# The recurrence's joint visits taken apart into the steps around them, and the decay rows spread over the partitions

## Chip, cores and metric

The kernel runs on one core of one Trainium2 chip. The metric is the device time of one execution in microseconds, the median over several; smaller is better.

## What is computed

A retention recurrence feeds a two-layer network. Batch 4, 8 heads, 768 tokens, head width 64; the network goes from 512 to 2048 and back to 512, on all 3072 tokens. The weights are handed over in double precision and made into fp32 on the chip.

```python
gamma = 1.0 - 2.0 ** (-5.0 - np.arange(H))
for t in range(S):
    state = gamma * state + einsum('bhd,bhe->bhde', k[:, :, t], v[:, :, t])
    y[:, :, t] = scale * einsum('bhd,bhde->bhe', q[:, :, t], state)
x = y.transpose(0, 2, 1, 3).reshape(B * S, H * D)
h = x @ w_in
g = np.maximum(0.01 * h, h)
out = g @ w_out
```

## The kernel before

**Chunks.** The 768 tokens are cut into NC = 6 chunks of 128 (`c`); each has 4 batches (`b`). For a chunk and batch the recurrence is a few small products on TensorE. `score` multiplies k by q into two PSUM banks (64x64 tiles of the array, four at a time); `masked` multiplies by the causal mask on VectorE. `decay_v` multiplies v by a power of the decay, on GpSimd, or on ScalarE and VectorE at the start. `reads` multiplies the state by q, `values` the masked scores by v, into the same two banks (`yp`); `state` multiplies k by v for the state's next value, into an unused part of those banks. `tokens_taken` moves the result into the network's input `x`, and `state_taken` adds the sums to the state and multiplies it by the decay; both are VectorE.

**The network.** Each matrix product is done with seven block products instead of eight (`seven`, steps M1, M6, M5, M4, M2, M7, M3), which land in the PSUM banks A, B, C, D, A, B, C of a ring of four (tag "ff"). `hidden(c, u)` is the first layer for a quarter `u` of the 2048 columns, `output` the second. A step of one part is 8 records of a 128x256 product on TensorE; in chunks 2 to 5 `output` takes two parts and 16 records. After each step VectorE or ScalarE empties the bank (`takes`): in `hidden`, M1 and M5 are copied by ScalarE, M6 is added by VectorE, M7 brings three VectorE adds and M3 one, and then the four differences of `g`. The seven products need differences of `x` as well (`differences`: four VectorE subtractions into `t` and `x[1]`); M1 needs none of them, M6 the second, M5 the first, M4 the third, M7 the changed `x[1]`.

**Order.** The order on every engine is that of the program text: each engine and each DMA queue works its list from front to back, and waits at an entry until what it depends on is done. `run(steps, at)` goes through the seven steps of a part and calls what `at` lists behind a step. Chunks 0 and 1 are worked together, unit by unit, while the weights arrive and are converted; chunks 2 to 5 follow one by one, each in two pairs of units (hidden, hidden, output).

**Where the recurrence of chunks 2 to 5 stands.** Behind chunk 0's last output part's steps 0 and 3 stand the scores and the rest for batches 0 and 1 of chunk 2 (`scored`, `visit`); step 4 of chunk 1's has the scores of batches 2 and 3. From then on `visit_with_scores` stands behind an output part: the scores of the next pair of batches (`score_apart`, each batch into two "ff" banks) between the reads, values and sums of the present pair, whose sums go into an "ff" bank of their own (`states_apart`). Where a chunk is completed by a visit, the differences of its `x` lie in it too. The last pair of batches has `visit` in output step 3.

**Loads.** SP's queue issues the loads of q and k (`ahead`, once the reads have let go of the old ones), then those of k and v (`load_kv`, at the visit's end), then the stores of the output parts. Batches 2 and 3 have their q and k in a free output tile.

**The start.** The decay tables come as 8 rows of 780 numbers in partitions 0 to 7 (`rows`, part of `t`), on ScalarE's DMA queue, and are spread over the partitions by products of 8 rows (`tables`, `spread`) into `dec`. Before data arrives TensorE multiplies zeros (`keep_busy`, from `nothing`, a 256-column strip of `t` set to zero by VectorE).

Of the kernel before, what the change touches and what calls it, by code (L numbers as in the profile page):

```python
# [23 lines left out]
def kernel(  # L24
# [143 lines left out]
    turn = [0]  # L168

    def new_am(c, b):  # L170

        i = turn[0]
        turn[0] = (i + 1) % (3 if (c, b) >= (2, 2) else 2)
        if i < 2:
            return work.tile([128, 2, HP, C], FP32, tag=f"am{i}", name=f"am_{c}_{b}")
        place = new_t(1, f"am_{c}_{b}").rearrange("p i k n -> p (i k n)")[:, 0 : 2 * HP * C]
        return place.rearrange("p (j a t) -> p j a t", j=2, a=HP)

    def new_t(c, name):
        return work.tile([128, 3, 2, N], FP32, tag=f"t{int(c == 1)}", name=name)  # L180

    def new_o(c, name="o"):
        return work.tile([128, 4, 2, N], FP32, tag=f"o{int(c > 0)}", name=f"{name}_{c}")

    def masked(c, b):
        am = new_am(c, b)
        nc.vector.tensor_tensor(
            out=am.rearrange("p j a t -> p (j a) t"),
            in0=scores[c, b].rearrange("p j a t -> p (j a) t"),
            in1=mask.unsqueeze(1).to_broadcast([128, H, C]), op=ALU.mult)  # L190
        scores[c, b] = am
# [25 lines left out]
    def state(c, b):  # L217
        y = heads[c, b][1]
        sp = for_state(sums_at[c, b])
        for a in range(HP) if c < NC - 1 else ():  # L220
            sums_of(sp, y, a)
# [24 lines left out]
    def taken(c, b, xb):  # L246

        tokens_taken(c, b, xb)
        state_taken(c, b, for_state(sums_at[c, b]))
# [7 lines left out]
    def state_taken(c, b, sp):  # L257
        sums_at.pop((c, b))
        if 0 < c < NC - 1:
            nc.vector.tensor_tensor(out=st[b], in0=st[b], in1=sp, op=ALU.add)  # L260
            nc.vector.tensor_tensor(out=st[b], in0=st[b],
                                    in1=gc.unsqueeze(2).to_broadcast([128, HP, D]), op=ALU.mult)

    def ahead(c, b):


        if c >= NC:
            return
        if b < 2:
            x = work.tile([128, 2, HP, C], FP32, tag="qk", bufs=AHEAD, name=f"qk_{c}_{b}")  # L270
        else:
            if b == 2:
                room[c] = new_o(0).rearrange("p i k n -> p (i k n)")
            x = room[c][:, ds((b - 2) * 2 * HP * C, 2 * HP * C)]
            x = x.rearrange("p (s a t) -> p s a t", s=2, a=HP)
        heads[c, b] = [x, None]
        load_qk(c, b)

    def load_kv(c, b):
        y = work.tile([128, 2, H, D], FP32, tag="kv", bufs=AHEAD, name=f"kv_{c}_{b}")  # L280
        heads[c, b][1] = y
        nc.sync.dma_start(out=y, in_=kv[c, b])

    room = {}

    def score_apart(c, b):

        x = heads[c, b][0]
        ps = scores[c, b] = [psum.tile([128, HP, C], FP32, tag="ff", bufs=4, name=f"ap{j}_{c}_{b}")
                             for j in range(2)]  # L290
        for a in range(HP):
            for u in range(2):
                for j in range(2):
                    nc.tensor.matmul(ps[j][ts(u, 64), a, :], lhsT=x[ts(j, 64), 1, a, ts(u, 64)],  # L294
                                     rhs=x[ts(j, 64), 0, a, :])

    def masked_apart(c, b, j):
        if j == 0:
            weights_of[c, b] = new_am(c, b)
        nc.vector.tensor_tensor(out=weights_of[c, b][:, j], in0=scores[c, b][j],  # L300
                                in1=mask.unsqueeze(1).to_broadcast([128, HP, C]), op=ALU.mult)
        if j == 1:
            scores[c, b] = weights_of.pop((c, b))

    weights_of = {}

    def states_apart(c, b):

        ps = psum.tile([128, 2, HP, D], FP32, tag="ff", bufs=4, name=f"sp_{c}_{b}")
        for i in range(2):  # L310
            y = heads.pop((c, b + i))[1]
            for a in range(HP):
                sums_of(ps[:, i], y, a, start=(i == 0 and a == 0))
        return ps

    def visit(c, b):

        for f in (reads, values, state):
            for i in range(2):
                f(c, b + i)  # L320
        for i in range(2):
            tokens_taken(c, b + i, xs[c][0])
        for i in range(2):
            state_taken(c, b + i, for_state(sums_at[c, b + i]))
        for i in range(2):
            if c + 1 < NC:
                ahead(c + 1, b + i)

    def visit_with_scores(c, b, following, complete=False):

        x = xs[c][0]
        early, late = ((following[0], following[1] + i) for i in range(2))
        score_apart(*early)
        for i in range(2):
            reads(c, b + i)
        masked_apart(*early, 0)
        masked_apart(*early, 1)
        score_apart(*late)  # L340
        for i in range(2):
            values(c, b + i)
        masked_apart(*late, 0)
        for i in range(2):
            tokens_taken(c, b + i, x)
        sp = states_apart(c, b)
        if complete:
            if xs[c][1] is None:
                xs[c][1] = new_t(c, f"t_{c}")
            t = xs[c][1]  # L350
            for k in range(2):
                minus(t[:, 0, k], x[:, 1, k], x[:, 0, k])
                minus(t[:, 1, k], x[:, 3, k], t[:, 0, k])
        masked_apart(*late, 1)
        if complete:
            minus(t[:, 2], x[:, 2], t[:, 1])
            last_difference(x)
        for i in range(2):
            state_taken(c, b + i, sp[:, i])
        for i in range(2):  # L360
            ahead(c + 1, b + i)
        for at in (early, late):
            load_kv(*at)
        for at in (early, late):
            decay_v(*at)
# [126 lines left out]
    def last_difference(x):  # L492
        minus(x[:, 1], x[:, 3], x[:, 1])
# [3 lines left out]
    FIRST = (0, 4, 1, 2, 3, 5, 6)  # L497
# [148 lines left out]
    def new_x(c):  # L646
        x = tile_x(c)
        return [x, new_t(c, f"t_{c}") if c < 3 else None]
# [22 lines left out]

    def differ(c):
        def do():
            if xs[c][1] is None:
                xs[c][1] = new_t(c, f"t_{c}")
            differences(*xs[c])
        return do
# [12 lines left out]
    place_for(0, 2, new_o(0, "in"))  # L690
    place_for(0, 3, new_o(1, "in"))
# [3 lines left out]
    rows = t[0:H, 1:3].rearrange("p i k n -> p (i k n)")[:, 0 : decay.shape[1]]  # L695
    nc.scalar.dma_start(out=rows, in_=decay)
# [27 lines left out]
    nothing = t[:, 0, 0, :].bitcast(BF16)  # L724
    nc.vector.memset(t[:, 0, 0, :], 0.0)
    idle = psum.tile([128, 2, N], FP32, tag="ff", bufs=4, name="idle")

    def keep_busy(n):
        for _ in range(n):
            nc.tensor.matmul(idle.rearrange("p i n -> p (i n)"), lhsT=nothing[:, 0:128],  # L730
                             rhs=nothing, start=True, stop=True, skip_group_check=True)
# [8 lines left out]
    keep_busy(7)  # L740
# [6 lines left out]
    nc.vector.tensor_copy(out=dec[:, n_gq:], in_=tables[:, 0, 0 : H + HP])  # L747
# [3 lines left out]
    decay_v(0, 0, nc.vector)  # L751
# [77 lines left out]
    later = hidden(1, 0, x1, t1, *parts[1][1:], order=FIRST)  # L829
# [9 lines left out]
    state_taken(1, 2, for_state(sums_at[1, 2]))  # L839
    state_taken(1, 3, for_state(sums_at[1, 3]))  # L840
# [4 lines left out]
    for u in range(NU):  # L845
# [5 lines left out]
        for c in range(2):  # L851
# [5 lines left out]
            if u == NU - 1 and NC > 2:  # L857
                if c == 0:
                    xs[2] = new_x(2)
                if c == 0:  # L860
                    at = {0: [scored(2, 0), scored(2, 1)], 3: [lambda: visit(2, 0)]}
                else:
                    at = {1: [lambda: ahead(2, 2), lambda: ahead(2, 3)],
                          2: [lambda: load_kv(2, 2), lambda: load_kv(2, 3)],
                          4: [scored(2, 2), scored(2, 3)]}
            run(output(c, os[c], [parts[c]], u == 0, u == NU - 1), at)

    if NC > 2:
        visit_with_scores(2, 2, (3, 0), complete=True)
    for c in range(2, NC):  # L870
        os[c] = new_o(c)
        for p in range(NU // 2):
            pair = []
            for u in (2 * p, 2 * p + 1):
                pair.append(new_g(c, u))
                run(hidden(c, u, *xs[c], *pair[-1][1:]), {})
            last = p == NU // 2 - 1
            at = {}
            if c + 2 == NC and last:
                at = {3: [lambda: visit(c + 1, 2)], 5: [differ(c + 1)]}  # L880
            run(output(c, os[c], pair, p == 0, last), at)

            if c + 1 < NC and p == 0:
                xs[c + 1] = new_x(c + 1)
                visit_with_scores(c + 1, 0, (c + 1, 2))
            elif c + 2 < NC and last:
                visit_with_scores(c + 1, 2, (c + 2, 0), complete=True)
# [83 lines left out]
```

## Time and profile before

| | |
|---|---|
| median of 3 runs | 667.42 us (666.89 to 667.49) |
| the profiled execution | 667.42 us, span 665.4 us |
| TensorE matmul, busy | 658.7 us |
| TensorE weight load, busy | 574.2 us |
| VectorE, busy | 372.1 us |
| ScalarE, busy | 176.2 us |
| GpSimd, busy | 18.5 us |
| granted TensorE clock | 1.00 |
| moved by DMA | 48.92 MB, mean 74 GB/s |

The span is the time from the first to the last instruction that the profiler shows; the execution's time has some 2 us around it. Busy time is the union of an engine's instructions. Matmuls overlap in the array, so that a row's busy time is longer than the distance between starts. In the timeline a row has: start in us, busy time in us, engine, line, operation, output<-inputs, shape, how many were merged, and in brackets the idle time of the engine before the row with what ended it. PE is TensorE, DVE VectorE, ACT ScalarE, POOL GpSimd; SPq is SP's DMA queue.

### The profile page before, as it was taken

Reading aid. Unit: us, or ns where it says so; the run is one execution under the profiler, and the core shown is the slowest. Engines: PE = TensorE matmul, PEld = TensorE weight load, DVE = VectorE, ACT = ScalarE, POOL = GpSimd, SP = SyncE. Lnnn points to the kernel's source line nnn. Section 1 sums busy time; section 2 is a strip of 40 time slices with the busy share of each in tenths; the row PEclk is TensorE's granted clock in tenths of the full one; section 3 lists DMA queues with packets and bytes.
Section 4 is the critical chain, followed back from the end, with each engine's and each line's share of the span. In section 5 each row is a group of like instructions: output and inputs, shape, how many; then the busy total and the mean of one; then the engine's idle time right before and its main releaser. Section 6 shows DMA issues by size and latency. Waiting matters only on the chain.

```text
span 665.4 us, 10517 instructions
## 1 busy us (share of the span) xinstructions
PE 658.7 (99%) x4537; PEld 574.2 (86%) x4537; DVE 372.1 (56%) x588; ACT 176.2 (26%) x322; POOL 18.5 (3%) x22
## 2 busy tenths in 40 slices
PE   8999999999999999999999999999999999999998
PEld 5888888888888888888888888888888888888886
DVE  5789969889888684243437414527333343431342
ACT  5854555264261002202102211300220210221210
POOL 0000000000000020001001001001000100000000
DMA  8920312313222640030022003004000101000001
GB/s 325 398 103 33 126 64 76 115 65 109 113 83 86 222 182 1 0 116 12 1 93 99 1 1 127 1 16 176 1 0 23 42 1 43 22 0 1 1 0 63
DMA packets 15757, 48.92 MB, mean 74 GB/s; under 512 B 1752, under 2 KB 2008, under 8 KB 15712
## 3 DMA queue, kind: packets, MB, share of 16 engines
q1 hardware_dynamic: 15696, 48.24, 20.0%
q8 instruction: 35, 0.57, 0.4%
q14 instruction: 10, 0.08, 0.0%
q10 hardware_dynamic: 16, 0.02, 0.0%
HBM read 41.97 MB, written 6.29 MB: 73 GB/s over the span
## 4 chain that ended last, share of the span: by engine, by line
PE 95%; DVE 2%; DMA 1%; SPq 0%; issue 0%
PE B_o L521 13%; PE A_o L521 13%; PE C_o L521 12%; PE A_h L521 12%; PE C_h L521 11%; PE B_h L521 11%; PE D_o L521 6%; PE D_h L521 6%; PE yp L210 3%; PE d L543 2%; PE ap L294 2%; PE ap L165 1%; PE yp L201 1%; DMA in<-in_qk_dram 1%; DVE t L470 1%; PE sp L225 1%
## 5 line engine op out<-in xcount | busy, mean ns | idle before, releaser
L521 PE MATMUL A_h<-x,w 128*128 128x256 f32 x368 | 87.7, 381 | 0.0
L521 PEld LDWEIGHTS A_h<-x,w 128*128 128x128 f32 x368 | 69.3, 190 | 9.7 <-issue 0.2
L521 PE MATMUL A_o<-g,w 128*128 128x256 f32 x288 | 68.1, 379 | 0.0
L467 DVE TENSOR_TENSOR m<-m,B_h 128x512 f32<-128x512 f32 x23 | 15.8, 687 | 90.8 <-PE B_h L521 90.8
L521 PEld LDWEIGHTS A_o<-g,w 128*128 128x128 f32 x288 | 54.6, 190 | 7.6 <-issue 0.2
L561 ACT COPY m<-A_h 128x512 f32<-128x512 f32 x23 | 13.5, 586 | 175.8 <-PE A_h L521 155.5
L556 ACT ACTIVATE g<-g 128x512 f32<-128x512 f32 x69 | 42.0, 629 | 66.0 <-DVE g L467 66.0
L467 DVE TENSOR_TENSOR m<-m,B_o 128x512 f32<-128x512 f32 x16 | 11.0, 685 | 64.3 <-PE B_o L521 64.3
L521 PE MATMUL D_h<-t,w 128*128 128x256 f32 x184 | 43.7, 380 | 0.7 <-DVE states L260 0.6
L521 PE MATMUL C_h<-x,w 128*128 128x256 f32 x184 | 43.5, 379 | 0.0
L521 PE MATMUL C_h<-t,w 128*128 128x256 f32 x184 | 43.5, 379 | 0.0
L521 PE MATMUL B_h<-t,w 128*128 128x256 f32 x184 | 43.5, 379 | 0.0
L521 PE MATMUL B_h<-x,w 128*128 128x256 f32 x184 | 43.5, 379 | 0.0
L521 PEld LDWEIGHTS D_h<-t,w 128*128 128x128 f32 x184 | 34.7, 190 | 6.4 <-PE C_h L521 1.8
L521 PEld LDWEIGHTS C_h<-x,w 128*128 128x128 f32 x184 | 35.0, 190 | 4.8
L521 PEld LDWEIGHTS C_h<-t,w 128*128 128x128 f32 x184 | 35.0, 190 | 4.8
L521 PEld LDWEIGHTS B_h<-t,w 128*128 128x128 f32 x184 | 35.0, 190 | 4.8
L521 PEld LDWEIGHTS B_h<-x,w 128*128 128x128 f32 x184 | 35.0, 190 | 4.7
L470 DVE TENSOR_TENSOR gd<-g,gd 128x512 f32<-128x512 f32 x48 | 33.2, 692 | 1.7
L521 PE MATMUL C_o<-gd,w 128*128 128x256 f32 x144 | 34.0, 379 | 0.0
L521 PE MATMUL B_o<-gd,w 128*128 128x256 f32 x144 | 34.0, 379 | 0.0
L521 PE MATMUL B_o<-g,w 128*128 128x256 f32 x144 | 34.0, 379 | 0.0
(125 smaller groups left out, 999.5 us busy)
## 6 DMA issues: line engine op xcount, KB each, us to landing
raw<-in_weights_dram SPq DMA_DIRECT2D x31, 512.0 KB, 4.3
kv<-in_kv_dram SPq DMA_DIRECT2D x17, 512.0 KB, 4.7
out_dram<-o SPq DMA_DIRECT2D x23, 256.0 KB, 2.3
qk<-in_qk_dram SPq DMA_DIRECT2D x11, 512.0 KB, 3.6
o<-in_qk_dram SPq DMA_DIRECT2D x8, 512.0 KB, 3.3
in<-in_qk_dram SPq DMA_DIRECT2D x5, 512.0 KB, 8.6
in<-in_kv_dram SPq DMA_DIRECT2D x3, 512.0 KB, 8.4
kv<-in_kv_dram SPq DMA_DIRECT2D x4, 256.0 KB, 7.2
```

The costliest lines, as they stand in the source:

```text
L165: nc.tensor.matmul(ps[ts(u, 64), j, a, :], lhsT=x[ts(j, 64), 1, a, ts(u, 64)], rhs=x[ts(j, 64), 0, a, :])
L201: nc.tensor.matmul(ps[ts(i, 64), j, m, :], lhsT=st[b][ts(j, 64), a, :], rhs=x[ts(j, 64), 0, a, :], start=(m == 0), stop=False, skip_group_ ...
L210: nc.tensor.matmul(ps[ts(i, 64), j, m, :], lhsT=y[:, 1, 2 * a + j, :], rhs=am[:, j, a, :], start=(c == 0 and m == 0), stop=True, skip_grou ...
L225: nc.tensor.matmul(sp[ts(j, 64), a, :], lhsT=y[:, 0, 2 * a + j, :], rhs=y[:, 1, 2 * a + j, :], start=start, stop=True, skip_group_check=True)
L294: nc.tensor.matmul(ps[j][ts(u, 64), a, :], lhsT=x[ts(j, 64), 1, a, ts(u, 64)], rhs=x[ts(j, 64), 0, a, :])
L467: nc.vector.tensor_tensor(out=out, in0=a, in1=b, op=ALU.add)
L470: nc.vector.tensor_tensor(out=out, in0=a, in1=b, op=ALU.subtract)
L521: nc.tensor.matmul(half, lhsT=block(w, sa)[:, k, ts(i, 128)], rhs=rhs[:, k, :], start=(first and (i == 0 or split) and n == 0 and k == 0), ...
L543: nc.tensor.matmul(banks[r][:, i, :], lhsT=block(2 * u, r + 2 * kh)[:, k, ts(i, 128)], rhs=x[:, 2 * kh + th, k, :], start=(step == 0 and i ...
L556: nc.scalar.activation(g[:, i], g[:, i], AF.Prelu, alpha=0.01)
L561: nc.scalar.copy(out=got["m1"], in_=ps)
```

## The change

The joint visits go. For each chunk from 2 on, the scores of a pair of batches stand behind one step and reads, values, sums, tokens and state behind a later one: in output steps 0 and 3 of chunks 0 and 1 for chunk 2, and in steps 1 and 4 of the first hidden part of each pair for chunks 3 to 5. Both use the two-bank tiles (tag "att"). The loads of the pair after the next two batches are issued right behind a read, q and k and then k and v for each batch. The differences of chunk 2 stand in output step 4 of chunk 1, the others in output step 1 of the second pair.

At the start the 8 rows lie in partitions 0, 16, 32 and so on, and GpSimd and VectorE first set all 128 partitions of that strip to zero, so that the products that spread them run over 128 rows. `nothing` is 64 columns wide, set before all else on VectorE; eight products of zeros stand at the front in place of seven. ScalarE copies the small table to `dec`, and GpSimd makes the first `decay_v`.

```diff
-    def visit(c, b):
+    def products(c, bs):
         for f in (reads, values, state):
-            for i in range(2):
-                f(c, b + i)
...
+            for b in bs:
+                f(c, b)
+
+    def stage_y(c, bs, xb):
+        products(c, bs)
+        for b in bs:
+            taken(c, b, xb)
+            n = c * B + b + AHEAD
+            if c > 1 and n < NC * B:
+                load(*divmod(n, B))
...
-    def visit_with_scores(c, b, following, complete=False):
...
+    def read(c, *bs):
+        return lambda: stage_y(c, bs, xs[c][0])
...
-    rows = t[0:H, 1:3].rearrange("p i k n -> p (i k n)")[:, 0 : decay.shape[1]]
-    nc.scalar.dma_start(out=rows, in_=decay)
+    rows = t[:, 1:3].rearrange("p i k n -> p (i k n)")[:, 0 : decay.shape[1]]
+    nothing = t[:, 0, 0, 0:64].bitcast(BF16)
+    nc.vector.memset(t[:, 0, 0, 0:64], 0.0)
+    half = decay.shape[1] // 2
+    nc.gpsimd.memset(rows[:, :half], 0.0)
+    nc.vector.memset(rows[:, half:], 0.0)
+    nc.scalar.dma_start(out=rows[0 : 128 : 128 // H], in_=decay)
...
-    nothing = t[:, 0, 0, :].bitcast(BF16)
-    nc.vector.memset(t[:, 0, 0, :], 0.0)
...
-            nc.tensor.matmul(idle.rearrange("p i n -> p (i n)"), lhsT=nothing[:, 0:128],
-                             rhs=nothing, start=True, stop=True, skip_group_check=True)
+            nc.tensor.matmul(idle.rearrange("p i (two n) -> p (i two) n", two=2), lhsT=nothing,
+                             rhs=nothing.unsqueeze(1).to_broadcast([128, 4, 128]),
+                             start=True, stop=True, skip_group_check=True)
...
-    keep_busy(7)
+    keep_busy(8)
...
-    nc.vector.tensor_copy(out=dec[:, n_gq:], in_=tables[:, 0, 0 : H + HP])
+    nc.scalar.copy(out=dec[:, n_gq:], in_=tables[:, 0, 0 : H + HP])
...
-    decay_v(0, 0, nc.vector)
+    decay_v(0, 0)
...
-                if c == 0:
-                    at = {0: [scored(2, 0), scored(2, 1)], 3: [lambda: visit(2, 0)]}
-                else:
-                    at = {1: [lambda: ahead(2, 2), lambda: ahead(2, 3)],
-                          2: [lambda: load_kv(2, 2), lambda: load_kv(2, 3)],
-                          4: [scored(2, 2), scored(2, 3)]}
+                at = {0: [scored(2, 2 * c), scored(2, 2 * c + 1)],
+                      3: [read(2, 2 * c, 2 * c + 1)]}
+                if c == 1:
+                    put(at, s4=[differ(2)])
             run(output(c, os[c], [parts[c]], u == 0, u == NU - 1), at)
-    if NC > 2:
-        visit_with_scores(2, 2, (3, 0), complete=True)
     for c in range(2, NC):
+        more = c + 1 < NC
         os[c] = new_o(c)
+        if more:
+            xs[c + 1] = new_x(c + 1)
         for p in range(NU // 2):
             pair = []
             for u in (2 * p, 2 * p + 1):
                 pair.append(new_g(c, u))
-                run(hidden(c, u, *xs[c], *pair[-1][1:]), {})
-            last = p == NU // 2 - 1
-            at = {}
-            if c + 2 == NC and last:
-                at = {3: [lambda: visit(c + 1, 2)], 5: [differ(c + 1)]}
-            run(output(c, os[c], pair, p == 0, last), at)
-            if c + 1 < NC and p == 0:
-                xs[c + 1] = new_x(c + 1)
-                visit_with_scores(c + 1, 0, (c + 1, 2))
-            elif c + 2 < NC and last:
-                visit_with_scores(c + 1, 2, (c + 2, 0), complete=True)
+                at = {}
+                if more and u == 2 * p:
+                    at = {1: [scored(c + 1, u), scored(c + 1, u + 1)],
+                          4: [read(c + 1, u, u + 1)]}
+                run(hidden(c, u, *xs[c], *pair[-1][1:]), at)
+            at = {1: [differ(c + 1)]} if p == 1 and more else {}
+            run(output(c, os[c], pair, p == 0, p == NU // 2 - 1), at)
```

More of the change, by code (lines that the diff above doesn't have):

```diff
@@ L166, in score @@
                                      rhs=x[ts(j, 64), 0, a, :])
[L168 to L183, printed above, removed]
     def masked(c, b):
-        am = new_am(c, b)
+        am = work.tile([128, 2, HP, C], FP32, tag="am", bufs=2, name=f"am_{c}_{b}")
         nc.vector.tensor_tensor(
@@ L217, in state @@
     def state(c, b):
-        y = heads[c, b][1]
+        y = heads.pop((c, b))[1]
         sp = for_state(sums_at[c, b])
@@ L248, in taken @@
         tokens_taken(c, b, xb)
-        state_taken(c, b, for_state(sums_at[c, b]))
+        state_taken(c, b)
     def tokens_taken(c, b, xb):
@@ L255, in tokens_taken, with state_taken @@
         nc.vector.tensor_tensor(out=blocks, in0=ps[:, :, 0 : HP // 2, :], in1=gq, op=ALU.mult)
-    def state_taken(c, b, sp):
-        sums_at.pop((c, b))
+    def state_taken(c, b):
+        ps = sums_at.pop((c, b))
         if 0 < c < NC - 1:
-            nc.vector.tensor_tensor(out=st[b], in0=st[b], in1=sp, op=ALU.add)
+            nc.vector.tensor_tensor(out=st[b], in0=st[b], in1=for_state(ps), op=ALU.add)
             nc.vector.tensor_tensor(out=st[b], in0=st[b],
                                     in1=gc.unsqueeze(2).to_broadcast([128, HP, D]), op=ALU.mult)
[L264 to L270, printed above, removed]
-        else:
[L272 to L309, printed above, removed]
-        for i in range(2):
[L311 to L314, printed above, removed]
@@ L316, in visit @@
-    def visit(c, b):
-        for f in (reads, values, state):
-            for i in range(2):
-                f(c, b + i)
[L321 to L327, printed above, removed]
-    def visit_with_scores(c, b, following, complete=False):
[L333 to L365, printed above, removed]
@@ L496 @@
     ORDER = (0, 1, 2, 3, 4, 5, 6)
-    FIRST = (0, 4, 1, 2, 3, 5, 6)
     def seven(tiles, name, takes, takes_half=None, order=ORDER):
@@ L647, in new_x, with new_o @@
         x = tile_x(c)
-        return [x, new_t(c, f"t_{c}") if c < 3 else None]
+        t = work.tile([128, 3, 2, N], FP32, tag="t", bufs=2, name=f"t_{c}")
+        return x, t
+    def new_o(c):
+        return work.tile([128, 4, 2, N], FP32, tag="o", bufs=2, name=f"o_{c}")
     slot = [0]
@@ L670, in scored @@
         return do
+    def read(c, *bs):
+        return lambda: stage_y(c, bs, xs[c][0])
     def differ(c):
[L673 to L677, printed above, removed]
+        return lambda: differences(*xs[c])
     def put(at, **more):
@@ L689 @@
     place_for(0, 1)
-    place_for(0, 2, new_o(0, "in"))
-    place_for(0, 3, new_o(1, "in"))
+    place_for(0, 2, new_o("in2"))
+    place_for(0, 3, new_o("in3"))
     words = tile_x("words").rearrange("p i k n -> p (i k n)")[:, 0 : 2 * W]
@@ L828 @@
     scored_later(3)
-    later = hidden(1, 0, x1, t1, *parts[1][1:], order=FIRST)
+    later = hidden(1, 0, x1, t1, *parts[1][1:], order=(0, 4, 1, 2, 3, 5, 6))
     next(later)
@@ L838 @@
     differences(x1, t1)
-    state_taken(1, 2, for_state(sums_at[1, 2]))
-    state_taken(1, 3, for_state(sums_at[1, 3]))
+    state_taken(1, 2)
+    state_taken(1, 3)
     run(later, {0: [next_mantissas], 1: [lambda: differences(*parts[0][1:])],
@@ L859 @@
                     xs[2] = new_x(2)
-                if c == 0:
-                    at = {0: [scored(2, 0), scored(2, 1)], 3: [lambda: visit(2, 0)]}
-                else:
-                    at = {1: [lambda: ahead(2, 2), lambda: ahead(2, 3)],
-                          2: [lambda: load_kv(2, 2), lambda: load_kv(2, 3)],
-                          4: [scored(2, 2), scored(2, 3)]}
+                at = {0: [scored(2, 2 * c), scored(2, 2 * c + 1)],
+                      3: [read(2, 2 * c, 2 * c + 1)]}
+                if c == 1:
+                    put(at, s4=[differ(2)])
             run(output(c, os[c], [parts[c]], u == 0, u == NU - 1), at)
-    if NC > 2:
-        visit_with_scores(2, 2, (3, 0), complete=True)
     for c in range(2, NC):
+        more = c + 1 < NC
         os[c] = new_o(c)
+        if more:
+            xs[c + 1] = new_x(c + 1)
         for p in range(NU // 2):
```

## The prediction

> **What bounds the kernel now.** I read the page's busy table first, then the chain that ended last, then the timeline of TensorE's matmuls around the recurrence, then the same stretch with VectorE and GpSimd beside it, and the first 15 us last.
>
> ```profile
> PE 658.7 (99%) x4537; PEld 574.2 (86%) x4537; DVE 372.1 (56%) x588; ACT 176.2 (26%) x322; POOL 18.5 (3%) x22
> ...
> PE 95%; DVE 2%; DMA 1%; SPq 0%; issue 0%
> ```
>
> TensorE is busy 99% of the span and holds 95% of the chain; the other engines are at 56% and less. A busy matmul row can hide a wait, so I go by starts: eight records of a 128x256 step start 1.73 us apart from the next eight (243.46 to 245.19 below). Whatever lies between two such steps beyond 1.73 us is the price of what stands there. Nothing off TensorE counts unless it makes a matmul start late.
>
> The first lines below are a part of the recurrence set apart, as the kernel still does it behind the last unit of chunk 0: the scores of two batches, then later reads, values and sums. The second are a joint visit.
>
> ```profile
> 203.49 1.89 PE L521 MATMUL A_o<-g,last 128*128 128x256 f32 x8
> 205.31 1.98 PE L165 MATMUL ap<-qk 64*64 64x128 f32 x64
> ...
> 209.05 1.89 PE L521 MATMUL C_o<-gd,last 128*128 128x256 f32 x8
> 210.77 1.89 PE L521 MATMUL D_o<-gd,last 128*128 128x256 f32 x8
> 212.59 1.10 PE L201 MATMUL yp<-qk,states 64*64 64x128 f32 x32
> ...
> 215.42 1.10 PE L225 MATMUL yp<-kv 128*64 128x64 f32 x32
> ...
> 218.29 1.89 PE L521 MATMUL B_o<-g,last 128*128 128x256 f32 x8
> ```
>
> ```profile
> 287.15 3.62 PE L521 MATMUL C_o<-g,w 128*128 128x256 f32 x16
> ...
> 290.69 1.10 PE L294 MATMUL ap<-o 64*64 64x128 f32 x32
> ...
> 291.62 1.05 PE L201 MATMUL yp<-qk,states 64*64 64x128 f32 x32
> ...
> 295.27 1.10 PE L225 MATMUL sp<-kv 128*64 128x64 f32 x32
> ...
> 298.13 1.89 PE L521 MATMUL B_h<-t,w 128*128 128x256 f32 x8
> ```
>
> Joint: C_o should end at 287.15 + 3.45 = 290.60, and A_h, had it lost nothing, would have begun at 298.13 - 1.73 = 296.40: 5.80 us. Apart: scores from 203.49 + 1.73 = 205.22 to 209.05 - 1.73 = 207.32, 2.10 us; the rest from 212.50 to 218.29 - 1.73 = 216.56, 4.06 us; 6.16 us together.
>
> **The change, part by part.**
>
> *Where the recurrence stands.* Six joint visits (the one behind chunk 1, two behind parts of chunk 2, two of chunk 3, one of chunk 4) become twelve stretches set apart, between the steps of hidden and output parts. Each pays 6.16 - 5.80 = 0.36 us more: one more way in and out of the small tiles, and a change of tile shape ahead of the reads. 6 x 0.36 = **+2.2**. The rows show this on TensorE in both forms, so I take it as it is.
>
> The Trainium skill, TensorEngine Tiling (Array Packing), Key Properties, says that changing the tiling mode drains TensorE. It gives no time, so no sum follows from it; it speaks against this change, and by it too each added stretch costs.
>
> *Sums that nobody uses.* states_apart makes the state sums without asking for the chunk, also for batches 0 and 1 of the last chunk, whose state is never read. state asks (c < NC - 1). So one pair of batches loses its 32 sum products. The read of batches 2 and 3 of the last chunk, already without sums, runs in the trace from 551.90 to 555.03, 3.13 us against 4.06: **-0.93**.
>
> *The wait behind the three joint visits that complete a chunk.* There the fourth bank of the next hidden part waits for the second addition into the state, since states_apart's bank comes round to it:
>
> ```profile
> 243.46 1.89 PE L521 MATMUL B_h<-t,w 128*128 128x256 f32 x8
> ...
> 245.19 1.89 PE L521 MATMUL C_h<-t,w 128*128 128x256 f32 x8
> ...
> 245.56 1.04 POOL L147 TENSOR_TENSOR kv<-kv,dec 128x512 f32<-128x512 f32 x1 [10.74 <-DMA kv<-in_kv_dram]
> 245.71 1.17 DVE L261 TENSOR_TENSOR states<-states,dec 128x256 f32<-128x256 f32 x1
> 246.80 0.41 DVE L260 TENSOR_TENSOR states<-states,sp 128x256 f32<-128x256 f32 x1
> ...
> 247.36 1.97 PE L521 MATMUL D_h<-t,w 128*128 128x256 f32 x8 [0.28 <-DVE states L260]
> ```
>
> From C_h's start to that of the next A_h (at 249.16, the row after these) are 3.97 us where two steps need 3.45: 0.52 lost. At 354.01 and 462.88 the same two steps take 4.01 and 3.79: 0.56 and 0.34. With the new places the sums lie in the "att" banks, the differences follow a part later: **-1.4**.
>
> *A new wait, in one place.* After the change the read of batches 2 and 3 of chunk 2 stands in output step 3 of chunk 1, and the four differences of chunk 2 in step 4, ahead in VectorE's queue of the add that empties bank B (step 5) and of the three adds behind it, the last of which empties bank C. Call T the start of step 4's matmuls. From the read at 212.59 (T = 216.45): VectorE ends the tokens and states at T + 2.4, the o add at T + 3.1; four differences take 2.7 (564.07 to 566.80 in chunk 4's output), so T + 5.8; the add of bank B ends at T + 6.4, that of C at T + 8.4. The next hidden part wants B at 1.83 + 3 x 1.73 = T + 7.0 and C at T + 8.7. Alone it just fits. But the change also issues the next loads at once behind the read (qk, kv, qk, kv on SP's queue, ahead of the stores), and in the trace half a megabyte passes every 1.3 us, about 1 us after its issue: the two kv land near T + 2.4 and T + 5, and GpSimd's two products of 1.04 us fall among the differences. The lines above show what that does: L261, two SBUF inputs, took 1.17 us beside a GpSimd product (0.42 without); the L260 with a PSUM input took 0.41. One block of about 0.4 and one of 1.0 make B late by 0.4 to 1.0 and C by 0.2 more, up to 1.3 in all; 0 if the second kv lands after the adds. Nearest row: L261's, so I take **+1.0**, ends 0 and 1.3. If this cover is lost, what is late next is VectorE's u add of M6, due 5 us later and harmless.
>
> The Trainium skill, SBUF — State Buffer, "SBUF: two separate sides", calls the pair of ports that VectorE and GpSimd share an exclusive lock: whoever starts first holds it for the whole instruction, and the other waits. By that alone two products would add 2 x 1.04 = 2.1 us to VectorE's queue, 1.4 to 1.5 us of it on B; the rows say less, as the first falls half beside a PSUM add.
>
> *The other reads, in hidden step 4.* There VectorE ends tokens and states at T + 2.4 and the adds of B and C at T + 3.1 and T + 5.2; they are wanted at T + 5.3 and T + 7.0. A single block of 1.04 still fits, so 0. The scores stand 5.2 us of matmuls ahead of the read; masked needs 2.4 us of VectorE, decay_v 2 x 1.04 of GpSimd on loads tens of us old: 0. The two score stretches of chunk 3's first pair begin at T + 8.75, with their qk issued at T - 3.1 and T + 0.2, landing by T + 3.4: 0.
>
> *The start.* The zeros are 64 columns wide and set first on VectorE, so the idle products start some 0.35 us sooner (they waited for two memsets until 1.40), eight instead of seven. Two memsets of 390 columns stand ahead of ACT's DMA of the decay rows (bounds for each: 0.27 us, L725's 256 columns on VectorE, and 1.05 us, GpSimd's 512-column product), and two more entries on VectorE's queue stand before the mask. ACT, not VectorE, copies the small table, and GpSimd makes the first decay_v (1.05 against 0.69 us). What sets the start is none of this:
>
> ```profile
> 12.56 1.10 PE L165 MATMUL ap<-in 64*64 64x128 f32 x32 [0.95 <-DMA in<-in_qk_dram]
> ```
>
> TensorE waits 0.95 us for batch 2's qk, issued on SP at 3.84, behind everything SP issued before; SP's entries are unchanged. From there on it never stops. The rows are needed at 6.0, would be issued near 1.6 instead of 0.8 and land about 2.5 to 4; landing at 7.5 would still leave the second values done before 12.56. Cost 0, ends -0.46 (the time in which the packets of the 24.4 KB passed at the head of the queues, 1.74 to 2.2) and +0.5.
>
> **Sum.** 2.2 - 0.93 - 1.4 + 1.0 + 0 = +0.9 us on the profiled execution's 667.42 us (span 665.4, 2.0 around it), which is also the median. Forecast **668.3**.
>
> **Rivals.**
>
> A: the differences at chunk 1's end don't collide (GpSimd's products fall later). Then -0.1: **667.3**. For it: the kv behind 226.28 took 6.2 us to GpSimd's start; against: there two qk were ahead in the queue.
>
> B, slower: VectorE is too late in the reads of hidden step 4 too. Margin to bank C is 7.0 - 5.2 = 1.8 us; from two whole blocks (2.08 us) ahead of the g add on it decides, each of the five reads that is followed by loads then loses 0.3 us, and the first wait reaches 1.3: 2.2 - 0.93 - 1.4 + 1.3 + 1.5 = +2.7, **670.1**. For it: loads start right behind the read; against: the second kv lands near T + 5, when that add is nearly done.
>
> C, faster: the start is worth more than I give it, the loads all landing sooner by the 0.46 and the 0.95 of TensorE's wait filled as well: 667.3 - 1.4 = **665.9**. Against it: the wait is for bytes, whose order and amount are the same.
>
> D: the tables land past 7.5 us, since the rows wait for two engines' memsets. One us later moves the direct products by as much: **669.3**.
>
> **How the numbers follow.** Forecast 0.55, A 0.16, B 0.17, C 0.06, D 0.06. 0.2% is 1.33 us, about what a measurement of this kernel can tell from no change. C is faster; B and D are slower, with some 0.07 of the forecast's own spread (0.6 us about 668.3 would pass 668.75). Faster 0.06, same 0.64, slower 0.30. The range 666.9 to 669.5 takes in A, the ends of the new wait (667.3 to 668.6) with those of the start, and D.
>
> **What would show it.** In the profile after: no D_h late by more than 0.1 us; L225 with 32 records fewer; each score stretch 2.1 and each read 4.06 us, the last two 3.13; the first B_h or C_h of chunk 2 late by about 1 us with a GpSimd product over the L470 differences; the third score stretch still at 12.5 us. A wait in every hidden part behind a read would make me wrong, and so would a third score stretch that starts elsewhere.

## The result and the profile after

| | before | after |
|---|---|---|
| median | 667.15 us (666.15 to 670.05, 6 runs) | 672.74 us (671.79 to 673.46, 6 runs) |
| profiled execution | 667.42 us, span 665.4 us | 672.50 us, span 670.4 us |
| first matmul of zeros | 1.40 us | 7.45 us |
| third score stretch | 12.56 us | 16.92 us |
| first direct product (`d`) | 14.25 us | 19.17 us |
| last matmul record starts | 661.87 us | 666.83 us |

The ratio is 1.0079 (1.0058 to 1.0100): the changed kernel is slower by 5.3 us in the means and 5.6 in the medians, and outside the predicted range. The last two rows of the table say where. From the first direct product to the last matmul record the kernel takes 661.87 - 14.25 = 647.62 us before and 666.83 - 19.17 = 647.66 after. Against this profile of before, everything that the change does to the recurrence nets to 0.04 us there; the 5 us stand ahead of it, in the first 19 us.

The page of the changed kernel, its busy table and the shares of its chain of waits:

```profile
PE 659.3 (98%) x4506; PEld 572.5 (85%) x4506; DVE 371.6 (55%) x569; ACT 175.7 (26%) x323; POOL 21.1 (3%) x24
...
PE 98%; DMA 1%; DVE 0%; issue 0%; DVEq 0%
```

TensorE is as busy as it was, in a longer span. The longest piece of the chain in order of time (start, length, what) is now the DMA of the decay rows:

```profile
1.50 5.81 DMA t<-decay_dram
```

TensorE's timeline of the first 20 us says who waits for it:

```profile
7.45 3.44 PE L629 MATMUL idle<-t 128*128 128x512 bf16 x8 [7.45 <-DMA t<-decay_dram]
10.82 1.10 PE L165 MATMUL ap<-qk 64*64 64x128 f32 x32
...
16.92 1.10 PE L165 MATMUL ap<-o_in 64*64 64x128 f32 x32
...
19.17 1.13 PE L436 MATMUL d<-x,w 128*128 128x256 f32 x4 [0.39 <-DVE w L357]
```

The bracket of the first row is the finding. The products of zeros read only the strip that VectorE clears, and VectorE has cleared it by 1.00 (start 0.89, 0.11 us). But they wait for the DMA that brings the decay rows into other columns of the same tile `t`, which lands at 1.50 + 5.81 = 7.31. The zeros, meant to fill the time until data arrives, come after the data: the first scores wait behind 10.82 - 7.45 = 3.4 us of products of nothing, though their q and k are there by some 4.6 (`no_zeros` and `own_zeros`, below, start the same scores on that DMA at 4.59 and 4.64).

The steps at chunk 1's last output part and behind it, on all engines, are those that the prediction's new wait was about (SPq rows and weight loads left out):

```profile
242.90 0.68 DVE L364 TENSOR_TENSOR t<-x 128x512 f32<-128x512 f32 x1
...
243.01 1.47 POOL L147 TENSOR_TENSOR kv<-kv,dec 128x512 f32<-128x512 f32 x1 [14.26 <-DMA kv<-in_kv_dram]
...
245.15 1.89 PE L414 MATMUL A_h<-x,w 128*128 128x256 f32 x8
...
246.28 0.68 DVE L361 TENSOR_TENSOR m<-m,B_o 128x512 f32<-128x512 f32 x1
...
246.88 1.89 PE L414 MATMUL B_h<-t,w 128*128 128x256 f32 x8
...
247.94 1.26 POOL L147 TENSOR_TENSOR kv<-kv,dec 128x512 f32<-128x512 f32 x1 [3.45 <-DMA kv<-in_kv_dram]
...
248.69 1.98 PE L165 MATMUL ap<-qk 64*64 64x128 f32 x64
...
250.60 1.99 PE L414 MATMUL C_h<-t,w 128*128 128x256 f32 x8
...
252.43 1.89 PE L414 MATMUL D_h<-t,w 128*128 128x256 f32 x8
```

B_h starts 246.88 - 245.15 = 1.73 us after A_h: no wait. From its end at 248.61 to where C_h would start without its change of tile shape (252.43 - 1.73 = 250.70) are 2.09 us, the price of the score stretch alone. D_h starts 1.83 us after C_h, of which 0.10 is the change of tile shape: no wait either.

### The profile page after: what moved, and what is told of

It is laid out like the page before. It is cut to its first block, busy times and chain, and to the rows that moved or that the text cites. A ratio compares the mean times of both kernels' runs of the same rounds, so it can differ in the third digit from the quotient of the medians.

```text
span 670.4 us, 10409 instructions
## 1 busy us (share of the span) xinstructions
PE 659.3 (98%) x4506; PEld 572.5 (85%) x4506; DVE 371.6 (55%) x569; ACT 175.7 (26%) x323; POOL 21.1 (3%) x24
## 4 chain that ended last, share of the span: by engine, by line
PE 98%; DMA 1%; DVE 0%; issue 0%; DVEq 0%
PE B_o L414 12%; PE A_o L414 12%; PE C_o L414 12%; PE C_h L414 12%; PE B_h L414 12%; PE A_h L414 12%; PE D_o L414 6%; PE D_h L414 6%; PE yp L193 3%; PE ap L165 3%; PE d L436 2%; PE yp L184 2%; PE yp L208 1%; DMA t<-decay_dram 1%; PE idle L629 1%; PE sums L208 0%
## 5 line engine op out<-in xcount | busy, mean ns | idle before, releaser
L238 DVE TENSOR_TENSOR x<-yp,dec 128x512 f32<-128x512 f32 x24 | 16.4, 689 | 50.6 <-PE yp L208 36.1
L170 DVE TENSOR_TENSOR am<-ap,mask 128x1024 f32<-128x1024 f32 x24 | 28.5, 1220 | 17.1 <-PE ap L165 17.1
L364 DVE TENSOR_TENSOR gd<-g,gd 128x512 f32<-128x512 f32 x48 | 35.4, 737 | 1.7
L147 POOL TENSOR_TENSOR kv<-kv,dec 128x512 f32<-128x512 f32 x18 | 20.2, 1125 | 463.3 <-DMA kv<-in_kv_dram 258.8
```

What stands on the lines that cost most here:

```text
L147: engine.tensor_tensor(out=v, in0=v, in1=gk.unsqueeze(2).to_broadcast([128, H, D]), op=ALU.mult)
L170: nc.vector.tensor_tensor(out=am.rearrange("p j a t -> p (j a) t"), in0=scores[c, b].rearrange("p j a t -> p (j a) t"), in1=mask.unsqueeze ...
L238: nc.vector.tensor_tensor(out=blocks, in0=ps[:, :, 0 : HP // 2, :], in1=gq, op=ALU.mult)
L364: nc.vector.tensor_tensor(out=out, in0=a, in1=b, op=ALU.subtract)
```

## The experiments

In each, "start" means the zeroed strip, the spread rows, the eight products of zeros and who copies the tables; "visits" means where the recurrence stands.

**The two halves of the change.** `visits_only` is the changed kernel with the start of before; `start_only` is the kernel before with the start of the change. The edits are the diff's hunks, taken apart.

> The recurrence's new places with the start of before. Theory S (the whole loss lies in the start: the products of zeros wait for the decay rows): first product of zeros at 1.4 us, third score stretch at 12.5, last product 0.2 us sooner than before; total 0 to 0.3 us below before, 667.0. Rival V (the twelve set-apart stretches cost the 5 us and the late start is hidden): total 671 to 673 as in the changed kernel.

> The joint visits of before with the new start. Theory S: first product of zeros near 7.4 us behind the DMA of the decay rows, third score stretch near 16.9 instead of 12.55, first direct product near 19.2 instead of 14.25; total 4.9 to 5.3 us above before, 672.2. Rival V: total within 0.7 us of before.

`visits_only` took 667.07 us against 666.62 of before, ratio 1.0009 (0.9998 to 1.0020); `start_only` 671.50 us, ratio 1.0068 (1.0054 to 1.0082). TensorE's first rows, of `start_only`:

```profile
7.03 3.57 PE L733 MATMUL idle<-t 128*128 128x512 bf16 x8 [7.03 <-DMA t<-decay_dram]
```

and a later one of `visits_only`:

```profile
14.60 1.67 PE L436 MATMUL d<-x,w 128*128 128x256 f32 x7
```

The start carries the loss, 4.88 us in the medians, with the same wait. From the first direct product to the last matmul record `visits_only` needs 662.02 - 14.60 = 647.42 us, 0.20 less than the profiled execution of before. Yet its median is 0.45 above that of before, where 0 to 0.3 below was expected; the interval holds both. Why the one profile flatters it is said further down.

**Is it the wait, or the late tables?** `own_zeros` is the changed kernel with the zeros in a tile of their own; the DMA, the memsets and the spread rows stay.

```diff
-    nothing = t[:, 0, 0, 0:64].bitcast(BF16)
-    nc.vector.memset(t[:, 0, 0, 0:64], 0.0)
+    zeros = work.tile([128, 2, N], FP32, tag="m1", name="zeros")[:, 0, 0:64]
+    nothing = zeros.bitcast(BF16)
+    nc.vector.memset(zeros, 0.0)
```

> The changed kernel, with the zeros in a tile that shares nothing with the decay rows. Theory S1 (the loss is the shared tile: the products of zeros, 3.4 us, stand behind a landing that they don't need): zeros start at 1.05 us, first scores at 4.6, tables wait for the rows to 7.4, third score stretch at 12.5 to 13.2, total 667 to 668. Rival S2 (the late landing of the rows alone does it, through the tables): third score stretch after 15, total 670 to 672.

667.66 us, ratio to before 1.0020 (1.0008 to 1.0032). TensorE at the start:

```profile
1.05 3.19 PE L630 MATMUL idle<-zeros 128*128 128x512 bf16 x8 [1.05 <-DVE zeros L594]
...
7.17 0.36 PE L644 MATMUL tables<-t 128*128 128x8 f32 x2 [1.43 <-DMA t<-decay_dram]
...
12.65 1.10 PE L165 MATMUL ap<-o_in 64*64 64x128 f32 x32 [0.37 <-DMA o_in<-in_qk_dram]
```

The zeros start at 1.05, 0.35 us before those of the kernel before. The rows land about as late as they did, and the tables wait 1.43 us for them until 7.17, yet the third score stretch starts at 12.65 on its own data. So the late landing alone is nearly covered, and what costs 5 us is that the zeros wait for it. What stays is small: `d` at 14.46 against 14.25, and 0.24 us behind it, traced below. Freed of the wait, the kernel is still 1.0 us slower than before in the medians.

**Does sharing the tile suffice?** `late_rows` is the kernel before, its 8 rows in partitions 0 to 7 as they were, but cleared first, so that their DMA goes out late as in the change.

```diff
+    half = decay.shape[1] // 2
+    nc.gpsimd.memset(rows[:, :half], 0.0)
+    nc.vector.memset(rows[:, half:], 0.0)
     nc.scalar.dma_start(out=rows, in_=decay)
```

> The kernel before with its rows in partitions 0 to 7, but set to zero first by GpSimd and VectorE in halves as in the changed kernel, so that their DMA is issued at 1.5 instead of 0.8 us. The zeros stay in the same tile. Theory Q: packets after 5 us, landing near 7. Theory F (the wait of the products of zeros comes from the strided partitions, whose span covers the zeros, not from the tile): zeros start at 1.8 us, tables wait to 7.2, third score stretch at 12.5 to 12.9, total within 1 us of before. Rival (sharing the tile is enough): zeros start after 7 us, total 5 us above before. Rival P: landing by 3.

667.32 us against 666.80, ratio 0.9999 (0.9980 to 1.0019). TensorE:

```profile
1.80 3.17 PE L733 MATMUL idle<-t 128*128 128x512 bf16 x7 [1.80 <-DVE t L728]
...
5.93 0.38 PE L745 MATMUL tables<-t 8*128 8x8 f32 x2
```

Here too the strip of zeros and the destination of the DMA share the tile, and the matmuls wait for VectorE only. So sharing the tile is not enough. What is left as the likely cause is the destination in every sixteenth partition, which the program then takes to overlap the strip. This is argued and not isolated: `late_rows` also clears its strip behind the DMA's issue and has it 256 columns wide, and whether the step or the reach over all partitions does it was not told apart. The rows, issued at 1.42, have their first packets at 3.92, their last by 4.72, and hold nobody up; the expected landing near 7 did not come.

**Why do the spread rows land so late?** `probe` is the kernel before with one more DMA: the rows, spread, into a tile that nobody reads, first in ScalarE's queue.

```diff
+    spare = work.tile([128, 4, 2, N], FP32, tag="g0", name="spare")
+    spare = spare.rearrange("p i k n -> p (i k n)")[:, 0 : decay.shape[1]]
+    nc.scalar.dma_start(out=spare[0 : 128 : 128 // H], in_=decay)
     nc.scalar.dma_start(out=rows, in_=decay)
```

> The kernel before with one DMA more, first on ScalarE's queue and with no wait: the decay rows into every sixteenth partition of a tile that nobody reads; the real rows follow as its second DMA. Theory Q (a DMA issued later stands behind the bytes that SP has issued by then): first packets at 1.7 us and landing by 2.5 to 3.5 for the spread rows, the second DMA's packets some us later. Rival P (spread partitions land slowly): the spread rows themselves land after 5 us although issued at 0.8.

One execution: 668.71 us. ScalarE's queue:

```profile
0.80 1.19 ACTq L698 DMA_DIRECT2D spare<-decay_dram  x1
2.03 0.34 ACTq L699 DMA_DIRECT2D t<-decay_dram  x1
```

The spread form keeps the queue 1.19 us, the contiguous one 0.34 here and 0.57 at the queue's head. Issued at 0.80, the contiguous rows of before have their first packets at 1.74, the spread ones at 3.41. The contiguous ones issued at 1.42 have theirs at 3.92, those issued at 2.03 at 5.98, and the spread ones of the changed kernel, issued at 1.50, at 5.7. By the end of the issue the five fall nearly into one order: ends at 1.37, 1.99, 1.99, 2.37 and 2.67 have first packets at 1.74, 3.41, 3.92, 5.98 and 5.7. So the longer issue counts as well as its later start. That the packets then stand behind the bytes which SP's queue has put in by then fits, but no run took SP's loads away. Neither theory was right as stated: the spread rows land by 4.4 here, not by 3.5 and not after 5.

**What if nobody multiplies zeros?** `no_zeros` leaves the eight products out of the changed kernel's start.

```diff
-    keep_busy(8)
```

> The changed kernel without its eight products of zeros at the front (they write nothing that is read). Theory S1: the scores no longer stand behind them, start at 4.6 us on the slow clock (32 records in about 2.0 us instead of 1.1), tables at 7.2, third score stretch at 13 to 14, total 667.5 to 669. Rival S2 (the landing alone costs): third score stretch after 15, total 670 or more.

670.51 us, ratio 1.0049 (1.0031 to 1.0066): the expectation of a start regained was missed. TensorE:

```profile
4.59 1.99 PE L165 MATMUL ap<-qk 64*64 64x128 f32 x32 [4.59 <-DMA qk<-in_qk_dram]
...
9.68 1.99 PE L165 MATMUL ap<-qk 64*64 64x128 f32 x32
...
14.54 1.10 PE L165 MATMUL ap<-o_in 64*64 64x128 f32 x32
```

The first scores start at 4.59, on time, but 32 records take 1.99 us where they take 1.10 in `own_zeros`, and so do those at 9.68. The array runs at about half its rate until some 13 us (the trace's record of a full clock begins at 12.82, in `own_zeros` at 3.71), and the third score stretch comes 14.54 - 12.65 = 1.9 us later than in `own_zeros`. The zeros are worth having, if they start early.

**The two terms of the visits that gain.** The kernel before was given the two gains without the new places. `no_last_sums` leaves out the state sums of the last chunk, whose result nobody reads; `adds_first` does both additions into the state ahead of both multiplications, so that the bank is free earlier; `both_kept` has both.

```diff
-            for a in range(HP):
+            for a in range(HP) if c < NC - 1 else ():
...
+        for i in range(2) if c < NC - 1 else ():
+            nc.vector.tensor_tensor(out=st[b + i], in0=st[b + i], in1=sp[:, i], op=ALU.add)
...
-            state_taken(c, b + i, sp[:, i])
+            sums_at.pop((c, b + i))
+        for i in range(2) if c < NC - 1 else ():
+            nc.vector.tensor_tensor(out=st[b + i], in0=st[b + i],
+                                    in1=gc.unsqueeze(2).to_broadcast([128, HP, D]), op=ALU.mult)
```

> The kernel before with two small edits: no state sums for the last chunk, and the two additions into the state ahead of the two multiplications in a joint visit. By the terms of the prediction -0.9 to -1.0 us for the sums and -1.4 for the wait of the fourth bank: 2.3 below before, 664.8; no step from C_h to D_h longer than 1.75 us. Rival: the additions, moved ahead, change nothing since GpSimd's product blocks VectorE anyway: -0.9 alone, 666.2.

> The kernel before with the two additions into the state ahead of the two multiplications in a joint visit, nothing else. Theory W (the wait of the fourth bank depends on when the kv land, and some executions of before lack it): no long step from C_h to D_h in the profile, the median 0.4 to 1.0 us below before, not 1.4. Rival: the wait is in every execution of before, so 1.4 us.

> The kernel before without the state sums of the last chunk's batches 0 and 1, nothing else. A term that cannot vary: the visit of these batches 0.9 to 1.0 us shorter in the profile, the median 0.9 to 1.0 us below before. Rival: TensorE's gain is given back to a wait for the tokens of the next hidden part: 0 to 0.4.

| | median | before beside it | ratio |
|---|---|---|---|
| `both_kept` | 665.03 us | 666.62 us | 0.9976 (0.9967 to 0.9985) |
| `adds_first` | 665.95 us | 666.83 us | 0.9974 (0.9957 to 0.9991) |
| `no_last_sums` | 665.43 us | 666.83 us | 0.9982 (0.9963 to 1.0001) |

The profiled execution of `adds_first` took 3288 us for a reason unknown, so that only its other times are used. The interval of `no_last_sums` just takes in no gain, but its profile shows the term: the visit of those batches takes 511.78 - 507.10 = 4.68 us instead of 513.81 - 508.20 = 5.61. `both_kept` beats both kernels, by 1.6 us over before in the medians; 2.3 were expected. Its main stretch, first direct product to last matmul record, takes 659.20 - 13.92 = 645.28 us, 647.62 - 645.28 = 2.34 less than the first profile of before, which is the sum of the two terms, 0.93 and 1.42, to 0.01. Around the first visit that completes a chunk:

```profile
245.52 1.04 POOL L147 TENSOR_TENSOR kv<-kv,dec 128x512 f32<-128x512 f32 x1 [11.42 <-DMA kv<-in_kv_dram]
245.60 1.58 DVE L363 TENSOR_TENSOR states<-states,dec 128x256 f32<-128x256 f32 x2
...
246.59 1.89 PE L526 MATMUL D_h<-t,w 128*128 128x256 f32 x8
```

VectorE's multiplications still meet GpSimd (1.58 us for two, otherwise 0.42 each), but nobody waits for them: D_h starts on time.

**Are the waits of the fourth bank always there?** Some profiles of other variants lacked them. `before_look_1` and `before_look_2` are the kernel before, unchanged, profiled twice more.

> The kernel before once more. Theory W: the three steps from C_h to D_h lose other amounts than the 0.44, 0.48 and 0.26 us of the first profile, at least one of them none. Rival: the same three amounts to 0.05 us.

> As the look before it: under theory W other amounts again, under the rival the same three.

They took 666.06 and 669.58 us. From C_h's start to that of the next A_h, beyond 3.45 us, the first profile loses 0.52, 0.56 and 0.34 us; `before_look_1` has one such wait, of 0.31, and `before_look_2` one, of 0.65. The place that the prediction showed, in `before_look_1`:

```profile
246.10 0.41 DVE L260 TENSOR_TENSOR states<-states,sp 128x256 f32<-128x256 f32 x1
...
246.47 1.04 POOL L147 TENSOR_TENSOR kv<-kv,dec 128x512 f32<-128x512 f32 x1 [11.28 <-DMA kv<-in_kv_dram]
...
246.96 1.89 PE L521 MATMUL D_h<-t,w 128*128 128x256 f32 x8
```

GpSimd starts at 246.47, once its load has landed, behind the second addition instead of ahead of the first multiplication as at 245.56 in the first profile. A landing 0.9 us later in one DMA decides over half a microsecond of TensorE. And in `before_look_2`, TensorE's start:

```profile
4.67 1.98 PE L165 MATMUL ap<-qk 64*64 64x128 f32 x32
...
7.45 2.05 PE L748 MATMUL spread<-t 8*128 8x512 f32 x2
9.43 1.99 PE L165 MATMUL ap<-qk 64*64 64x128 f32 x32
```

This is the half rate of `no_zeros`, in a kernel without any edit, with its seven products of zeros in place from 1.39: `d` starts at 17.21 instead of 14.25. The first scores alone do not tell: `before_look_1` has 1.99 us there too, but 1.10 from the second scores at 8.25 on, and its `d` starts at 14.15. The same start of the same kernel can cost 3 us more from one execution to the next.

## Why the prediction was wrong

| term | predicted, us | measured, us |
|---|---|---|
| the start | 0 (-0.46 to +0.5) | +4.92 up to `d`, 0.24 behind it |
| twelve stretches for six visits | +2.2 | scores 2.09 + rest 4.05 = 6.14 against 6.16 supposed |
| sums that nobody uses | -0.93 | 3.12 for the last reads against 4.05: -0.93 |
| the fourth bank's waits | -1.4 | -1.42 against the first profile; -0.31 and -0.65 against the other two |
| the new wait at chunk 1's end | +1.0 (0 to 1.3) | 0 |

**The step that failed** is the start's: "What sets the start is none of this", with its cost of 0 and its idle products "some 0.35 us sooner". It priced the zeros by VectorE's queue and the rows by when the tables are needed, and never asked what else the products of zeros wait for now that the rows' destination has changed form. They wait for the DMA; 7.45 us instead of 1.05. `own_zeros`, which takes only this wait away, starts its zeros at 1.05 as the prediction had it, and its third scores at 12.65 as the prediction had it: the reasoning on what covers the rows was right, for a kernel in which the zeros are free. The diff does not show this wait; TensorE's first row in the profile after does. The prediction had named the sign itself, a third score stretch that starts elsewhere than at 12.5: it starts at 16.92.

**The landing of the rows** was a miss of its own. They were put at 2.5 to 4 us and land at 7.31. The estimate took a late issue to cost only its delay. In the runs 0.6 us later at the queue's head means 2.2 us later first packets for the contiguous form (0.80 to 1.42; 1.74 to 3.92), and the spread form takes 1.16 to 1.19 us to issue instead of 0.57. Rival D named late tables, but with the price of a delay of the tables alone (669.3); the zeros were not in it, nor in the range.

**The new wait of +1.0 did not come**, so rival A's price was right on the visits, though only half of its condition held. GpSimd's products began 3.15 and 8.1 us after T = 239.86, where T + 2.4 and T + 5 were expected: the kv were issued at 239.54 and 241.12, and GpSimd began 3.5 and 6.8 us later. The first product did collide with the differences, took 1.47 us, and stretched the four to 3.5 us instead of 2.7; the second came behind the adds that matter. The margin of 0.6 us took up the one collision. The add that empties bank B (246.28, 0.68 us) ends with B_h's start at 246.88, give or take the 0.09 us by which VectorE's rows overlap: just in time. For bank C the sum was wrong in the text itself: it let C_h follow B_h at T + 8.7, and forgot that the change puts the scores of chunk 3 between the two (the paragraph on the other reads has them there, at T + 8.75), which gives C 2.1 us more.

**The fourth bank's waits** are right in mechanism, and -1.42 in the execution that they were read from. But they are not a property of the kernel: the three profiles of before have 1.42, 0.31 and 0.65 us of them, 0.8 in the mean, and that of `start_only`, with the same visits, has none. That agrees with the medians of `adds_first` (0.88 lower); its ratio gives 0.6 to 2.9 us. The forecast took the dearest of the three as the price.

**The rest held.** The prices of the stretches and of the sums came out within 0.02 us. Without the new wait the prediction's terms give -0.13 on the visits, and `visits_only` has -0.20 over its main stretch. But both lean on the first profile of before. With 0.8 us for the fourth bank's waits the terms give 2.2 - 0.93 - 0.8 = +0.5, near the 0.45 by which the median of `visits_only` is above before: on the whole the new places seem to gain nothing, though that interval (-0.1 to +1.3 us) takes in no change.

That the changed kernel has +0.04 over its main stretch and not -0.20 comes with its start: `own_zeros` too takes 647.66. The 0.24 us lies in the first direct products. From `d` to the scores behind it they and one `values` take 23.98 - 19.17 = 4.81 us, 4.81 in `own_zeros` too, and 18.82 - 14.25 = 4.57 before, 4.57 in `visits_only`. The load of their weights waits for VectorE, which is still converting them, ahead of the first product and again half-way; before waits at neither place:

```profile
21.03 1.59 PEld L436 LDWEIGHTS d<-x,w 128*128 128x128 f32 x8 [0.27 <-DVE w L357]
```

## What to carry to other kernels

Ahead of pricing a start, read for the first entry of every engine's list what it waits for, and do not infer it from the columns that it reads alone: a filler is worth something only if it waits for nothing, so give it a tile that no transfer writes. A DMA to a few rows in spread partitions is not the same transfer as one to adjacent rows; its issue, its landing and what is taken to depend on it all change. And a wait of half a microsecond that hangs on which of two engines starts first has a price only as a mean over several profiles; a version that takes it away, with the unused sums left out, gave the 0.24% that the whole change was not able to keep.

## What the hardware showed that was not expected

- One DMA of 24.4 KB keeps its issuing queue 0.57 us for 8 adjacent partitions (0.34 as second DMA of the queue) and 1.16 to 1.19 us for 8 spread ones.
- At the start, with SP's queue filling the engines, 0.62 us of later issue became 2.18 us of later first packets, and 1.23 us of later issue (0.80 to 2.03) became 4.24 (1.74 to 5.98).
- TensorE's array can run at half rate far into the start: 32 score records in 1.99 us instead of 1.10, in `no_zeros` still at 9.68 and in `before_look_2`, without an edit, at 9.43. The profile's row of granted clock reads full there, but the trace holds no clock record of that time: its first, of a full clock, begins at 12.82 and at 14.12 us. In `probe` and `late_rows` the record shows the clock fall back to 0.50 for 3.41 us, from 9.67 and from 8.36 on. The Trainium skill, TensorE: Matmul & The Clock Gate, "Part 1: The HAM clock gate (the "warmup" mystery)", has the array at half its clock until a free-running window of some 3.4 us has been busy. The two rates, the 3.41 us and the change from execution to execution agree with that; that the slow part lasts some 8 us from the first scores on, more than two such windows, is not explained by it and stays open.
- VectorE's multiplication with two SBUF inputs took 0.43 us alone and 1.17 to 1.25 where it began just behind GpSimd's product (245.71 in before, 246.55 in `before_look_1`), and GpSimd's took 1.04 alone, and 1.26 to 1.47 where VectorE was first. The Trainium skill, SBUF — State Buffer, "SBUF: two separate sides", calls the shared ports a lock that the first to start holds; these rows agree in the main, on both sides; a full block would have made the 1.17 some 1.3 (GpSimd until 246.60, then 0.43).
